# Dense layer of a fused attention and mixture-of-experts kernel: weight conversion spread over other places of the activation, and the low operand's matmuls put last

## The chip, the cores and the metric

The kernel runs on one core of a Trainium2 chip. TensorE (PE) multiplies matrices into PSUM banks, VectorE (DVE), ScalarE (ACT) and GpSimd (POOL) work on elements, and SyncE (SP) issues most transfers. Each engine takes its own instructions in the order in which the program gives them, and waits for the others by semaphores. The metric is the device time of one execution in microseconds (us); lower is better.

## The reference

Three layers follow one another. The change lies in the second, which is dense:

```python
def _moe_ref(x, w_in, w_out):            # x: 1536 x 512, w_in: 512 x 2048, w_out: 2048 x 512
    h = x @ w_in
    beta = 1.0
    neg = h <= -beta
    pos = h >= beta
    g = np.where(pos, h, np.where(neg, 0.0, (h + beta) ** 2 / (4.0 * beta)))
    return (g @ w_out).astype(np.float32)
```

Ahead of it stands a bucketed attention that makes x (2 batches, 8 heads, 768 rows), and behind it a layer with 8 experts of which each token takes two.

## The kernel before

**Tiles and steps.** The 1536 tokens are cut into 4 chunks `c` of 384, and the 2048 hidden columns into 16 blocks `f` of 128. A step is one pair (c, f). The first 32 steps take chunks 0 and 1 in turn, so that block f is used in steps 2f and 2f+1; then chunk 2 takes its 16 blocks, then chunk 3. Every operand is held as two parts, a rounded high part and a low rest, so that a product is three matmuls: high by high, high by low, low by high.

**What a step does.** `hidden` (L552) gives TensorE 12 matmuls of 384 columns into one of two banks (L561; the third of them is the first that reads the low part `w[:, 1]` of the block's weights). Then the activation goes from engine to engine: ACT `relu` into `ga` (L567), DVE `clip` of `ga` (L570, both inputs in SBUF), DVE `max` of the bank and `ga` (L573, one input in PSUM), ACT `round` into the high part `gh` (L574), POOL `rest` into the low part `gl` (L575). `out` (L578) belongs to the step two earlier (`lag = 2`) and gives TensorE 9 matmuls of 512 columns (L584): for each of three output banks `gh` by high, `gh` by low, `gl` by high.

**Weight conversion.** The weights arrive as 64-bit words in `R`. They are turned into the two float parts in eight pieces (`Weights.steps`, L299), which go through a scratch tile `TB` with two halves, block j using half j mod 2: ACT `abs` (L315), DVE `clamp` (L316), DVE `shift` (L317), four DVE `merges` (L311), and the `split`, which is an ACT copy (L307) and a POOL subtraction (L308) that writes the low part. Blocks 0 to 2 are converted during attention. Blocks j = 3 to 15 are converted within the dense steps; block j starts at step s = 2j-4. So each pair of steps carries one whole conversion beside two activations.

**Order.** The order on every engine is that in which the Python code emits instructions; there is no scheduler. Steps 0 and 1 are emitted among the last instructions of attention. Before the change `hidden` takes one list `extra` and cuts it: its first two pieces go behind `relu`, the third behind `clip`, and those left behind `rest`. Even step s carries the first seven pieces, and odd step s+1 the split.

Of the kernel before, what the change touches and what calls it, by code (L numbers as in the profile page):

```python
# [47 lines left out]
def cols(i, n):  # L48
    return slice(i * n, (i + 1) * n)
# [19 lines left out]
class Attention:  # L69
# [175 lines left out]
    def run(self, hooks, drain):  # L245

        lag, nt, plan = 4, self.nt, {}
        for a in range(2):
            for i, j in enumerate((1, 1, 2, 3 + 4 * a, 3, 4)):
                plan.setdefault(j + 4 * a, []).append((self.prep, a, i))  # L250
            plan.setdefault(5 + 6 * a, []).append((self.proj, a, f"x{a}"))
        self.start()
        done = 0
        for t in range(nt + 4):
            pr, j = divmod(t, 12)
            if t < nt:
                self.scores(t)
            if t >= lag:
                self.transposes(t - lag)
            self.soft(t)  # L260
            self.flush(2 if j < 2 else 1)
            if pr < 7:
                for f, a, i in plan.get(j, []):
                    f(2 * pr + 2 + a, i)
            if pr < 8 and j == 0:
                self.load_v(pr)
            if pr < 6 and j in (6, 11):
                self.load(2 * pr + 4 + (j == 11))
            for f in hooks.get(t, []):
                f()  # L270
            if t >= lag + 6:
                self.values(*divmod(t - lag - 6, 6))
                done += 1
            if t >= nt:
                drain(t - nt)
        while done < nt:
            self.values(*divmod(done, 6))
            done += 1
        self.flush()
# [263 lines left out]
class Dense:  # L543
# [8 lines left out]
    def py(self, c):  # L552
        return self.banks[5:8] if c == 1 else self.banks[2:5]

    def hidden(self, i, c, f, extra):
        nc, p, w = self.nc, self.banks[i % 2][:, :HT], self.wt.W[f]
        V, A = nc.vector, nc.scalar
        n = 0
        for k in range(4):
            for a, x in ((0, 0), (0, 1), (1, 0)):  # L560
                nc.tensor.matmul(p, w[:, a, cols(k, 128)], self.X[c][:, x, k], start=n == 0, stop=n == 11)  # L561
                n += 1
        a = self.sb.tile([128, HT], F32, name="ga", bufs=2)
        gh = self.sb.tile([128, HT], F32R, name="gh", bufs=3)
        gl = self.sb.tile([128, HT], F32R, name="gl", bufs=3)
        self.G[c, f] = gh, gl
        A.activation(a, p, AF.Relu, bias=self.half[:, 0:1], scale=0.5)  # L567
        for e in extra[:2]:
            e()
        V.scalar_tensor_tensor(a, a, 1.0, a, op0=ALU.min, op1=ALU.mult)  # L570
        for e in extra[2:3]:
            e()
        V.tensor_tensor(a, p, a, op=ALU.max)  # L573
        A.activation(gh, a, AF.Copy)  # L574
        nc.gpsimd.tensor_sub(gl, a, gh.bitcast(F32))  # L575
        for e in extra[3:]:
            e()

    def out(self, c, f):
        gh, gl = self.G.pop((c, f))  # L580
        w = self.wt.W[f]
        for t in range(3):
            for i, (g, a) in enumerate(((gh, 0), (gh, 1), (gl, 0))):
                self.nc.tensor.matmul(self.py(c)[t], g[:, cols(t, 128)], w[:, a, 512:1024],  # L584
                                      start=f == 0 and i == 0, stop=f == NF - 1 and i == 2)

    def run(self, convert, late, rows):

        lag, g, wt, yT = 2, self.gate, self.wt, self.yT
        order = [(c, f) for f in range(NF) for c in range(2)] + [(c, f) for c in (2, 3) for f in range(NF)]  # L590

        def stages(s, n):

            for t in range(n):
                at(s + t, lambda t=t: g.transposes(t, g.tp, yT))
                at(s + t + 1, lambda t=t: g.logits(t, yT))
            s += n
            for i, f in ((0, g.noise_a), (1, g.noise_b), (2, g.noise_c), (2, g.top2), (3, g.weights), (4, g.rank), (4, g.slot)):
                at(s + i, f)
            for t in range(n):  # L600
                at(s + 5 + t // 3, lambda t=t: g.hot(t))
                at(s + 6 + t // 3, lambda t=t: g.place(t))

        plan = {}

        def at(i, f):
            plan.setdefault(i, []).append(f)

        split = {}
        for i in range(4 * NF + lag):  # L610
            if i < 4 * NF:
                extra = []
                for j in [j for j, s in convert.items() if s == i]:
                    st = wt.steps(j)
                    extra += st[:-1]
                    split.setdefault(i + 1, []).append(st[-1])
                extra += split.get(i, [])
                self.hidden(i, *order[i], extra)
            if i >= lag:
                c, f = order[i - lag]  # L620
                self.out(c, f)
                if f == NF - 1 and 0 < c < 3:
                    if c == 1:
                        g.take(0, rows(0))
                        for t in range(6):
                            g.evac(t, self.banks[2 + t])
                        stages(i + 1, 6)
                    else:
                        g.take(6, rows(2))
                        for t in range(3):  # L630
                            g.evac(t, self.py(2)[t])
                        stages(i + 1, 3)
            for e in plan.pop(i, []) + late.get(i, []):
                e()
            yield i


class Experts:
# [10 lines left out]
    def __init__(self, nc, tc, ident, gate, W, prefetch, banks, xd, idx, out, TB, XT):  # L649
        self.nc, self.tc, self.ident, self.gate, self.W, self.prefetch = nc, tc, ident, gate, W, prefetch  # L650
        self.xd, self.idx, self.dst, self.banks = xd, idx, out, banks
        self.V, self.A, self.G, self.T = nc.vector, nc.scalar, nc.gpsimd, nc.tensor
        flat = TB.rearrange("p a b -> p (a b)")
        self.xr = [flat[:, cols(b, XW)] for b in range(3)]
        self.XT = [XT]
# [102 lines left out]
    def rows(self, j, o):  # L758

        n, il, sent = self.blocks(j, o), self.il[o % 2], []  # L760
        gt = self.columns(j, o)[1]

        def one(b):
            if b == 0:
                self.V.tensor_tensor(il[:, :n], self.idx[:, self.col(j, 3 * o, n)], self.apart[:, :n], op=ALU.max)
            self.put(b, gt[:, b:b + 1], il[:, b:b + 1], sent)
        return [lambda b=b: one(b) for b in range(n)]
# [77 lines left out]

@with_exitstack
def tile_bucketed_attention__then__moe__then__moe2(ctx, tc, qk, vv, pp, wio, wg, wn, noise, w12, out):
    nc = tc.nc
    const = ctx.enter_context(tc.tile_pool(name="const", bufs=1))
# [177 lines left out]
```

## Time and profile before

| what | value |
|---|---|
| time, median of 3 runs (lowest to highest) | 961.88 us (960.09 to 964.64) |
| the profiled execution's own time | 965.52 us |
| its span on the core | 963.7 us, so 1.8 us lie around the span |
| busy share of the span: PE, DVE, ACT, POOL | 91%, 60%, 45%, 41% |
| dense steps 2 to 63 | 263.6 to 562.6 us |
| weight conversion within the dense steps (L307 to L317) | 266.6 to 393.9 us |

The busy shares are means over the whole span, so they hide a stretch in which another engine leads. PE's busy time counts overlapping matmuls and does not say that it runs at its peak.

### The profile page before, as it was taken

Reading aid. Unit: us, or ns where it says so; the run is one execution under the profiler, and the core shown is the slowest. Engines: PE = TensorE matmul, PEld = TensorE weight load, DVE = VectorE, ACT = ScalarE, POOL = GpSimd, SP = SyncE. Lnnn points to the kernel's source line nnn. Section 1 sums busy time; section 2 is a strip of 40 time slices with the busy share of each in tenths; the row PEclk is TensorE's granted clock in tenths of the full one; section 3 lists DMA queues with packets and bytes.
Section 4 is the critical chain, followed back from the end, with each engine's and each line's share of the span. In section 5 each row is a group of like instructions: output and inputs, shape, how many; then the busy total and the mean of one; then the engine's idle time right before and its main releaser. Section 6 shows DMA issues by size and latency. Waiting matters only on the chain.

```text
span 963.7 us, 13751 instructions
## 1 busy us (share of the span) xinstructions
PE 875.0 (91%) x4846; PEld 716.0 (74%) x4846; DVE 579.7 (60%) x1215; ACT 433.1 (45%) x786; POOL 393.8 (41%) x403
## 2 busy tenths in 40 slices
PE   5999999999999898999999999978988968989873
PEld 3666666666687777899899888867877857878763
DVE  7899999988378787532926725326333445354352
ACT  4787787788534434333334432214322334334240
POOL 7777776784244545322221320332123143140332
PEclk8999999999999999999999999979999979999987
DMA  4439212112560000000501421346535376483742
GB/s 148 157 107 265 83 50 83 50 50 94 201 274 1 1 0 1 1 1 1 198 1 63 145 69 36 70 81 159 165 79 134 124 213 167 164 223 101 202 91 37
DMA packets 39883, 98.49 MB, mean 102 GB/s; under 512 B 6080, under 2 KB 15296, under 8 KB 37696
## 3 DMA queue, kind: packets, MB, share of 16 engines
q1 hardware_dynamic: 30688, 73.69, 22.8%
q0 software_dynamic: 8912, 22.50, 11.2%
q8 instruction: 94, 1.54, 0.7%
q14 instruction: 45, 0.37, 0.1%
q10 hardware_dynamic: 144, 0.39, 0.1%
HBM read 80.00 MB, written 16.58 MB: 100 GB/s over the span
## 4 chain that ended last, share of the span: by engine, by line
PE 40%; DMA 33%; DVE 15%; ACT 5%; issue 3%; another core or an unknown queue 2%; POOL 1%; POOLq 0%; SPq 0%; ACTq 0%; DVEq 0%
DMA xr<-xd,idx 16%; DMA out_dram<-yT,il 9%; DMA xm<-xd,idx 8%; PE b L561 7%; PE b L584 7%; PE bank_x L217 6%; PE bank_t L209 5%; PE s L178 4%; DVE TB L311 4%; PE s L180 3%; DVE ga L570 2%; DVE st L189 2%; PE b L714 2%; PE b L720 2%
## 5 line engine op out<-in xcount | busy, mean ns | idle before, releaser
L714 PE MATMUL b<-W,hT 128*128 128x512 f32 x648 | 176.9, 416 | 39.3 <-issue 34.6
L714 PEld LDWEIGHTS b<-W,hT 128*128 128x128 f32 x648 | 122.6, 198 | 65.7 <-issue 41.5
L688 POOL DMA_INDIRECT out_dram<-yT,il x33 | 52.4, 1589 | 258.9 <-DVE yT L752 256.4
L748 DVE SCALAR_TENSOR_TENSOR hT<-b,hT 128x384 fp32r<-128x384 f32 x88 | 49.0, 556 | 178.8 <-ACT hT L747 177.2
L747 ACT ACTIVATE hT<-b 128x384 fp32r<-128x384 f32 x88 | 43.3, 492 | 236.2 <-PE b L720 235.5
L561 PE MATMUL b<-X,W 128*128 128x384 f32 x768 | 147.3, 340 | 0.0
L575 POOL TENSOR_TENSOR gl<-ga,gh 128x384 fp32r<-128x384 f32 x64 | 75.2, 1177 | 165.2 <-ACT gh L574 126.5
L561 PEld LDWEIGHTS b<-X,W 128*128 128x128 f32 x768 | 135.0, 189 | 6.2 <-issue 1.8
L200 POOL TENSOR_SCALAR p<-p,st 128x768 f32<-128x768 f32 x96 | 98.1, 1022 | 63.1 <-DVE st L195 51.4
L584 PE MATMUL b<-W,gh 128*128 128x512 f32 x384 | 120.7, 395 | 0.0
L197 ACT ACTIVATE p<-s,st 128x768 f32<-128x768 f32 x96 | 95.5, 995 | 41.7 <-DVE st L195 34.6
L189 DVE TENSOR_REDUCE st<-s 128x1 f32<-128x768 f32 x96 | 91.7, 955 | 17.7 <-PE s L180 16.1
L720 PEld LDWEIGHTS b<-XT,W 128*128 128x128 f32 x576 | 88.9, 197 | 5.3 <-issue 1.8
L720 PE MATMUL b<-XT,W 128*128 128x256 f32 (+2 forms) x576 | 91.7, 314 | 1.2 <-issue 1.1
L570 DVE SCALAR_TENSOR_TENSOR ga<-ga 128x384 f32<-128x384 f32 x64 | 46.9, 733 | 74.8 <-ACT ga L567 74.8
L932 DVE TENSOR_TENSOR W<-stage,W 128x1024 fp32r<-128x1024 f32 x64 | 78.3, 1224 | 22.0 <-ACT W L931 22.0
L584 PE MATMUL b<-W,gl 128*128 128x512 f32 x192 | 77.6, 404 | 12.8 <-POOL gl L575 12.8
L210 ACT ACTIVATE pT<-bank_t 128x384 f32<-128x384 f32 x192 | 83.4, 488 | 8.9 <-PE bank_t L209 7.9
L217 PE MATMUL bank_x<-pT,vt 128*64 128x384 f32 x384 | 81.8, 510 | 0.4 <-DVE KM L165 0.3
L720 PE MATMUL b<-XA,W 128*128 128x384 f32 (+1 forms) x480 | 81.5, 323 | 0.0
L574 ACT ACTIVATE gh<-ga 128x384 fp32r<-128x384 f32 x64 | 33.6, 525 | 105.9 <-DVE ga L573 105.9
L209 PE MATMUL bank_t<-ident,p 128*128 128x128 f32 x576 | 79.4, 274 | 1.4 <-ACT pT L210 1.4
(171 smaller groups left out, 1303.3 us busy)
## 6 DMA issues: line engine op xcount, KB each, us to landing
stage<-in_w_dram SPq DMA_DIRECT2D x64, 512.0 KB, 4.4
R<-in_wio_dram SPq DMA_DIRECT2D x16, 1024.0 KB, 7.3
raw<-in_qk_dram SPq DMA_DIRECT2D x15, 768.0 KB, 4.3
out_dram<-z SPq DMA_DIRECT2D x15, 256.0 KB, 4.9
vt<-in_vv_dram SPq DMA_DIRECT2D x8, 384.0 KB, 4.8
xd<-TB SPq DMA_DIRECT2D x3, 780.0 KB, 3.7
xd<-z SPq DMA_DIRECT2D x3, 260.0 KB, 6.0
xd<-rows SPq DMA_DIRECT2D x1, 780.0 KB, 6.0
```

The source lines that it names most:

```text
L189: V.tensor_reduce(st[:, 0:1], s[:, :, :HT], axis=AX.XY, op=ALU.min)
L197: self.A.activation(p.rearrange("p (a b) -> p a b", a=2), s[:, :, :HT], AF.Exp, bias=st[:, 2:3], scale=st[:, 3:4], accum_out=st[:, 5:6])
L200: self.G.tensor_scalar(self.P[t - 1], self.P[t - 1], ps[:, 5:6], 1.0, op0=ALU.mult, op1=ALU.mult)
L209: self.T.transpose(b[:, cols(j, 128)], p[:, cols(3 * g + j, 128)], self.ident)
L210: self.A.activation(self.PT[u, s][:, cols(g, 3), cols(i, 128)], b[:, :HT].rearrange("p (j q) -> p j q", j=3), AF.Copy)
L217: self.T.matmul(xp[cols(s, 64), :HT], self.vt[pr][:, s, kt, :], self.PT[u, s][:, kt, :], start=kt == 0, stop=kt == 5)
L561: nc.tensor.matmul(p, w[:, a, cols(k, 128)], self.X[c][:, x, k], start=n == 0, stop=n == 11)
L575: nc.gpsimd.tensor_sub(gl, a, gh.bitcast(F32))
L584: self.nc.tensor.matmul(self.py(c)[t], g[:, cols(t, 128)], w[:, a, 512:1024], start=f == 0 and i == 0, stop=f == NF - 1 and i == 2)
L714: self.T.matmul(self.banks[2 + b], h[:, a, cols(b, 128)], w2[:, x, 512:1024], start=i == LAG and n == 0, stop=i == LAG + 7 and n == 2)
L720: self.T.matmul(p, w[:, a, cols(k, 128)], X[:, x, k, :N], start=n == 0, stop=n == 11)
L932: nc.vector.tensor_sub(w[:, 1], d, w[:, 0].bitcast(F32))
```

## The change

`hidden` takes four lists in place of one and runs them at four places: `early` ahead of `relu`, `amid` behind `relu`, `mid` behind `clip`, `late` behind `rest`. `run` hands the eight pieces of block j to steps s-1 to s+2: abs to step s-1 (amid), clamp to s (mid), shift to s+1 (late), the four merges to s+2 (early) and the split to s+2 (amid). In `out` the two loops change places.

```diff
-    def hidden(self, i, c, f, extra):
+    def hidden(self, i, c, f, early, amid, mid, late):
...
         self.G[c, f] = gh, gl
+        for e in early:
+            e()
         A.activation(a, p, AF.Relu, bias=self.half[:, 0:1], scale=0.5)
-        for e in extra[:2]:
+        for e in amid:
             e()
         V.scalar_tensor_tensor(a, a, 1.0, a, op0=ALU.min, op1=ALU.mult)
-        for e in extra[2:3]:
+        for e in mid:
             e()
         V.tensor_tensor(a, p, a, op=ALU.max)
         A.activation(gh, a, AF.Copy)
         nc.gpsimd.tensor_sub(gl, a, gh.bitcast(F32))
-        for e in extra[3:]:
+        for e in late:
             e()
...
-        for t in range(3):
-            for i, (g, a) in enumerate(((gh, 0), (gh, 1), (gl, 0))):
+        for i, (g, a) in enumerate(((gh, 0), (gh, 1), (gl, 0))):
+            for t in range(3):
                 self.nc.tensor.matmul(self.py(c)[t], g[:, cols(t, 128)], w[:, a, 512:1024],
...
+            for n, (d, place) in enumerate([(-1, 1), (0, 2), (1, 3), (2, 0), (2, 0), (2, 0), (2, 0), (2, 1)]):
+                conv.setdefault(s + d, ([], [], [], []))[place].append(lambda j=j, n=n: wt.steps(j)[n]())
```

Line numbers in the changed kernel are 2 higher from `relu` on (L569 relu, L572 clip, L575 max, L576 round, L577 rest, L586 the matmuls of `out`).

On DVE, steps 3 to 5 before the change (`b1` is the bank of odd steps, `b0` of even ones, `R4` the words of block 4):

```order
L570 SCALAR_TENSOR_TENSOR ga_3037<-ga_3037 128x384
L573 TENSOR_TENSOR ga_3037<-b1_2854,ga_3037 128x384
L316 TENSOR_SCALAR TB_72<-TB_72 128x1024
L570 SCALAR_TENSOR_TENSOR ga_3069<-ga_3069 128x384
L317 TENSOR_SCALAR TB_72<-TB_72 128x1024
L573 TENSOR_TENSOR ga_3069<-b0_2853,ga_3069 128x384
L311 SCALAR_TENSOR_TENSOR TB_72<-R4_2598,TB_72 128x512 x4
L570 SCALAR_TENSOR_TENSOR ga_3105<-ga_3105 128x384
L573 TENSOR_TENSOR ga_3105<-b1_2854,ga_3105 128x384
```

The clamp, shift and merges of block 4 all stand in the even step 4. On DVE in the changed kernel, steps 3 to 5:

```order
L572 SCALAR_TENSOR_TENSOR ga_3032<-ga_3032 128x384
L575 TENSOR_TENSOR ga_3032<-b1_2854,ga_3032 128x384
L317 TENSOR_SCALAR TB_72<-TB_72 128x1024
L311 SCALAR_TENSOR_TENSOR TB_72<-R3_2596,TB_72 128x512 x4
L572 SCALAR_TENSOR_TENSOR ga_3063<-ga_3063 128x384
L316 TENSOR_SCALAR TB_72<-TB_72 128x1024
L575 TENSOR_TENSOR ga_3063<-b0_2853,ga_3063 128x384
L572 SCALAR_TENSOR_TENSOR ga_3100<-ga_3100 128x384
L575 TENSOR_TENSOR ga_3100<-b1_2854,ga_3100 128x384
L317 TENSOR_SCALAR TB_72<-TB_72 128x1024
L311 SCALAR_TENSOR_TENSOR TB_72<-R4_2598,TB_72 128x512 x4
```

The shift and merges of block 4 have moved from the even step to behind the next odd one, and the clamp has moved from ahead of the clip to behind it.

On PE, `hidden` of step 8 and the `out` behind it before the change (W_3109 is the weights of block 4):

```order
L561 MATMUL b_2853<-X_68,W_3109 128x384 [waits DVE_49]
L561 MATMUL b_2853<-X_68,W_3109 128x384 x11
L584 MATMUL b_2855<-W_3041,gh 128x512 [waits Activation_49]
L584 MATMUL b_2855<-W_3041,gh 128x512
L584 MATMUL b_2855<-W_3041,gl 128x512 [waits Pool_49]
L584 MATMUL b_2856<-W_3041,gh 128x512 x2
L584 MATMUL b_2856<-W_3041,gl 128x512
L584 MATMUL b_2957<-W_3041,gh 128x512 x2
L584 MATMUL b_2957<-W_3041,gl 128x512
```

In the changed kernel the same place reads (W_3139 is the weights of block 4):

```order
L561 MATMUL b_2853<-X_68,W_3139 128x384 [waits DVE_49,Activation_49]
L561 MATMUL b_2853<-X_68,W_3139 128x384
L561 MATMUL b_2853<-X_68,W_3139 128x384 [waits Pool_49]
L561 MATMUL b_2853<-X_68,W_3139 128x384 x9
L586 MATMUL b_2855<-W_3071,gh 128x512 [waits Activation_49]
L586 MATMUL b_2856<-W_3071,gh 128x512
L586 MATMUL b_2958<-W_3071,gh 128x512
L586 MATMUL b_2855<-W_3071,gh 128x512
L586 MATMUL b_2856<-W_3071,gh 128x512
L586 MATMUL b_2958<-W_3071,gh 128x512
L586 MATMUL b_2855<-W_3071,gl 128x512 [waits Pool_49]
```

The wait of `out` for POOL has moved from its third matmul to its seventh, and `hidden` of an even step now has waits of its own for ACT (first matmul) and for POOL (third), which come from the split.

## Rows read from the trace of the kernel before

**Rows 1.** Waits from 262 to 405 us: who waited for whom, total us, times, longest.
```profile
PE b L584 <- POOL gl L575: 12.8, 12, 1.1
```

**Rows 2.** The chain of waits from 286 to 396 us, its share by line.
```profile
by line: DVE TB L311 29.4%; DVE ga L570 14.1%; DVE TB L316 10.4%; ACT TB L315 10.3%; ACT W L307 9.3%; issue 8.9%; ACT ga L567 5.7%; DVE ga L573 5.5%; PE b L584 4.5%; PE b L561 1.9%; DVE TB L317 0.6%; ACT gh L574 0.2%; ACTq L307 0.2%
```

**Rows 3.** Timeline of PE, `hidden` of steps 3, 4, 30: start, us, operation.
```profile
267.90 2.25 PE L561 MATMUL b<-X,W 128*128 128x384 f32 x12
272.07 2.25 PE L561 MATMUL b<-X,W 128*128 128x384 f32 x12
...
396.91 2.25 PE L561 MATMUL b<-X,W 128*128 128x384 f32 x12
```

**Rows 4.** Timeline of ACT, steps 9 and 10: start, us, [idle before <- releaser].
```profile
292.79 1.06 ACT L307 ACTIVATE W<-TB 128x1024 fp32r<-128x1024 f32 x1 [2.29 <-DVE TB L311]
293.79 0.53 ACT L574 ACTIVATE gh<-ga 128x384 fp32r<-128x384 f32 x1
294.22 0.57 ACT L567 ACTIVATE ga<-b,half 128x384 f32<-128x384 f32 x1
294.69 1.12 ACT L315 ACTIVATE TB<-R 128x1024 f32<-128x1024 f32 x1
```

**Rows 5.** Timeline of DVE, steps 9 to 11.
```profile
292.62 0.54 DVE L570 SCALAR_TENSOR_TENSOR ga<-ga 128x384 f32<-128x384 f32 x1
...
295.84 1.05 DVE L316 TENSOR_SCALAR TB<-TB 128x1024 f32<-128x1024 f32 x1 [2.08 <-ACT TB L315]
296.81 1.34 DVE L570 SCALAR_TENSOR_TENSOR ga<-ga 128x384 f32<-128x384 f32 x1
298.08 0.68 DVE L317 TENSOR_SCALAR TB<-TB 128x1024 int32<-128x1024 int32 x1
298.68 0.54 DVE L573 TENSOR_TENSOR ga<-b,ga 128x384 f32<-128x384 f32 x1
299.15 3.30 DVE L311 SCALAR_TENSOR_TENSOR TB<-R,TB 128x512 int32<-128x512 int32 x4
302.37 0.54 DVE L570 SCALAR_TENSOR_TENSOR ga<-ga 128x384 f32<-128x384 f32 x1
```

**Rows 6.** Timeline of POOL: the subtraction of the split in step 9.
```profile
293.93 2.41 POOL L308 TENSOR_TENSOR W<-TB,W 128x1024 fp32r<-128x1024 f32 x1 [2.38 <-ACT W L307]
```

**Rows 7.** Timeline of DVE in step 2, with POOL idle.
```profile
267.70 0.69 DVE L316 TENSOR_SCALAR TB<-TB 128x1024 f32<-128x1024 f32 x1 [2.87 <-ACT TB L315]
268.31 0.55 DVE L570 SCALAR_TENSOR_TENSOR ga<-ga 128x384 f32<-128x384 f32 x1
268.78 0.69 DVE L317 TENSOR_SCALAR TB<-TB 128x1024 int32<-128x1024 int32 x1
```

**Rows 8.** Timeline of POOL, ACT and DVE after the last split.
```profile
391.46 2.40 POOL L308 TENSOR_TENSOR W<-TB,W 128x1024 fp32r<-128x1024 f32 x1 [2.38 <-ACT W L307]
...
391.75 0.57 ACT L567 ACTIVATE ga<-b,half 128x384 f32<-128x384 f32 x1
392.35 1.93 DVE L570 SCALAR_TENSOR_TENSOR ga<-ga 128x384 f32<-128x384 f32 x1 [1.06 <-ACT ga L567]
...
393.82 1.31 POOL L575 TENSOR_TENSOR gl<-ga,gh 128x384 fp32r<-128x384 f32 x1
394.31 0.56 DVE L573 TENSOR_TENSOR ga<-b,ga 128x384 f32<-128x384 f32 x1
```

**Rows 9.** Timeline of PE, `out` of one step with no wait.
```profile
403.20 0.63 PE L584 MATMUL b<-W,gh 128*128 128x512 f32 x2
403.66 0.40 PE L584 MATMUL b<-W,gl 128*128 128x512 f32 x1
403.90 0.63 PE L584 MATMUL b<-W,gh 128*128 128x512 f32 x2
```

**Rows 10.** Stretches: us; busy PE, PEld, DVE, ACT, POOL; granted clock; DMA share, GB/s.
```profile
286.00:396.90 110.90, 98.10 (x476) 84.46 (x475) 87.39 (x113) 44.25 (x68) 60.01 (x36) 1.00 0.00 1
410.00:480.00 70.00, 70.00 (x400) 63.68 (x400) 33.87 (x113) 24.16 (x43) 15.24 (x15) 1.00 0.17 61
```

More of the change, by code (lines that the diff above doesn't have):

```diff
@@ L607, in at @@
             plan.setdefault(i, []).append(f)
-        split = {}
+        conv = {}
+        for j, s in convert.items():
+            for n, (d, place) in enumerate([(-1, 1), (0, 2), (1, 3), (2, 0), (2, 0), (2, 0), (2, 0), (2, 1)]):
+                conv.setdefault(s + d, ([], [], [], []))[place].append(lambda j=j, n=n: wt.steps(j)[n]())
         for i in range(4 * NF + lag):
             if i < 4 * NF:
[L612 to L618, printed above, removed]
+                self.hidden(i, *order[i], *conv.get(i, ([], [], [], [])))
             if i >= lag:
```

## The prediction

> **What bounds the kernel now.** I read the waits of the dense stretch first. TensorE, the busiest engine of the page, loses time there in one place: `out` waits for `gl` 12 times, 12.8 us in total [rows 1]. Taken alone this says that `gl` is taken too early, or that POOL is too slow. The chain of waits over the same stretch says otherwise: TensorE's lines hold only 4.5% and 1.9% of it, and the rest is DVE and ACT work on weights and activation [rows 2]. So I looked for a loop between these two engines, in the timelines of ACT and DVE over one pair of steps [rows 4, 5].
>
> It is there, and it closes. The split's copy starts at 292.79; behind it in ACT's queue come round (293.79), relu of the next even step (294.22) and abs of the next block (294.69). DVE has been idle for 2.08 us until that abs ends, then takes clamp (295.84), clip (296.81), shift (298.08), max (298.68), merges (299.15), and the next clip may issue at 302.37. The next split's copy needs these merges. From clip to clip, 292.62 to 302.37, that is **9.75 us for a pair of steps**. TensorE alone needs 4.17 us for a step (267.90 to 272.07) [rows 3], 8.34 for a pair. Its waits for `gl` are only where the loop's lateness reaches it: POOL's subtraction of the split stands ahead of `gl` in its queue.
>
> **The change part by part.** Nothing is added or removed; all instructions are moved.
>
> *Low operand last in `out`.* It lets `gl` come four matmuls later, 4 x 0.23 = 0.9 us in each step. While the loop sets the pace this only moves the waiting, so I count it at 0; it would count where `gl` alone is late. It costs bank changes: each matmul now goes to another bank than the one before, 9 changes a step against 3. Two matmuls into one bank start 0.46 us apart from the next change (403.20 to 403.66), the change itself 0.24 (403.66 to 403.90) [rows 9]: 0.23 against 0.24, at most 0.01 for a change, so 384 changes more (6 x 64 steps) cost between 0 and 3.8 us; nearest is 0, since the difference is the rounding of the rows.
>
> *The loop is cut.* abs moves to the odd step before, so clamp finds its input ready. DVE's 2.08 us of idle time go, and the split's copy no longer stands between merges and clamp. What is left is a new loop, and to find its length one row decides: clip at 392.35 took 1.93 us beside the split's subtraction on POOL, against 0.55 alone [rows 7, 8]. It ended 0.42 after POOL's end (393.86 to 394.28), and `rest`, which was asked for at 393.82, ended 0.85 after clip. The max that followed ran 0.56 beside that `rest`, its ordinary 0.54 [rows 5, 8]. So clip and POOL's work exclude each other, and max is free. Clamp shows the same (1.05 against 0.69), merges too: four take 3.22 from issue to issue (299.15 to 302.37) with a `rest` inside [rows 5, 7].
>
> Now a pair in the new order, with 0 where the merges have been issued and clip of the even step can start:
> - clip 0 to 0.47, clamp to 1.08 (spacings 0.47 and 0.61 [rows 7]), then max;
> - the split's copy starts 0.17 behind the clip's place (292.62 to 292.79), POOL's subtraction 1.14 later at 1.31 (292.79 to 293.93), and takes 2.41, to 3.72 [rows 4 to 6];
> - clip of the odd step has its relu by about 2.8, waits for POOL, and ends at 3.72 + 0.42 = 4.14;
> - `rest` of the even step ends at 4.14 + 0.85 = 4.99. Max runs beside it; shift is held until then, and has passed by about 5.5 (its spacing is 0.60: 298.08 to 298.68 [rows 5]);
> - the merges with the odd step's `rest` inside, 3.22: the next clip can start at **8.7**.
>
> So DVE and POOL together set 8.7 us a pair, a little over TensorE's 8.34 and 1.05 under the old loop. That shift is held has no row; the nearest is clamp, the same operation at the same size and time (0.69, 0.69 [rows 7]), which was held, so I take it as held. If it is not, it runs beside `rest`, the merges start near 5.2 and the pair is 8.4. The other end: if POOL takes `rest` directly behind the subtraction, clip of the odd step ends at 3.72 + 0.85 + 0.42 = 4.99, max and shift follow, merges start at 6.07 and the pair is 9.3.
>
> The Trainium skill, page SBUF — State Buffer, section "Who interferes with whom", names `tensor_scalar` among the DVE operations that can hold the port pair shared with GpSimd, for the whole instruction. By that rule shift is held and the pair is 8.7; were it exempt, 8.4. No run here shows a shift beside POOL work, so the rule stands on the side of the value that I took from clamp's row.
>
> *Where the lateness goes next.* The subtraction now runs in step 2j-2 and writes the low weights that `hidden` of step 2j reads in its third matmul; the order shows the new wait there. In TensorE's own pace that matmul comes 5.74 us after clip's undisturbed start (8.34 + 0.35 - 2.95, with clip 2.25 + 0.10 + 0.60 behind the start of `hidden` [rows 3, 8]). The subtraction is done at 3.72 + 0.05, so DVE may be 2.0 late before TensorE waits. It starts 0.7 late and gains 0.36 a pair, so from the fourth or fifth pair on `hidden` waits about 0.36 us a pair, 3 us in all. The seventh matmul of `out` needs `gl` of the even step at 4.99, long after: there is no wait there.
>
> **Sum.** Step 3's `hidden` starts at 267.90 as before; its relu follows at 270.25, clip 270.85, max 271.45, shift 271.92, merges 272.52, and with 3.22 the first clip behind merges is at 275.7. Twelve pairs of 8.7 later, at 380.1, the last block's merges are done. Its subtraction ends 3.72 later, and `hidden` of step 30 can start at 380.1 + 3.77 - 0.35 = 383.5. Before it started at 396.91 [rows 3]. **Gain 13.4 us.** TensorE is then back to back (70.00 busy of 70.00 from 410 to 480 [rows 10]) and the conversion is over, so I see nothing that takes the gain back. abs of block 3 moves into attention's end, where ACT waits for DVE's max anyway. Transfers hide nothing and delay nothing: from 286 us on they move 1 GB/s [rows 10]. From the profiled execution's 965.52 the sum gives 952.1; that execution lies 3.64 above the median of 961.88, from which it is **948.5 us**, the predicted time.
>
> **Rivals.**
> - *TensorE sets the pace* (shift free, pair 8.4). The lateness stays under 2.0, `hidden` of step 30 starts at 272.07 + 13 x 8.34 = 380.5, gain 16.4, 945.5 us. Against it: the port work has to fit with no gap.
> - *POOL keeps the port* (pair 9.3). The last merges are done at 275.7 + 12 x 9.3 = 387.3, step 30 starts at 390.7, gain 6.2, 955.7 us. Against it: at 393.86 the waiting clip went ahead of the queued `rest` [rows 8].
> - *No change.* The gain is made and given back behind step 33, for instance in the gathers of the expert layer: 960 to 964. Against it: no timed event stands there, only work that shifts as a whole.
> - *Slower: changing banks costs.* If each of the 384 added changes costs more than (13.4 + 4.8) / 384 = 0.047 us, the kernel is slower by over 0.5%; at 0.06 it loses 23 us, wins 13.4, and takes 971.5. Against it: 0.01 at most in [rows 9].
>
> **How the numbers follow.** Chances: forecast (pair 8.5 to 9.0) 0.62, TensorE's pace 0.14, POOL keeps the port 0.14, no change 0.07, slower 0.03. The forecast's own range is a pair of 8.5 to 9.0 (gain 16 to 9.8, up to 952.1) with 1.5 us of scatter between runs. The range 944.5 to 956 takes in the first two rivals and leaves out the others. A difference of 0.5% (4.8 us) is about what can be told from no change: faster 0.90, same 0.07, slower 0.03.
>
> **What would show it.** Right: merges start every 8.6 to 8.8 us; the wait of `out` for `gl` is under 1 us in total; a new one, the third matmul of `hidden` on POOL's L308, grows from mid-stretch to about 3 us; clip of the odd step takes about 1.3 us on average; step 30 starts near 383.5. Wrong: merges every 8.34 (shift free) or 9.3 (`rest` first), clamp still idle behind abs, DVE ops of one length beside POOL work, or `out` matmuls more than 0.24 apart.

## The result, and the profile after

The changed kernel took 952.76 us (median of 4 runs, 948.55 to 955.30) beside 961.82 us for the kernel before: a ratio of 0.990, 95% interval 0.985 to 0.994, so 9 us faster by the medians. The profiled execution took 953.94 us, its span is 952.2 us. Timed again beside the experiments (e4 below), the same kernel took 950.82 us against 963.16 us, a ratio of 0.987 (0.984 to 0.990), 12.3 us. The prediction was 948.5 us from a gain of 13.4 us; both intervals hold its ratio of 0.986.

Where the time came from is seen in `hidden` of steps 3 and 30, which answer to [rows 3]. The timeline of PE in the changed kernel:

```profile
264.14 2.35 PE L561 MATMUL b<-X,W 128*128 128x384 f32 x12
...
268.41 2.25 PE L561 MATMUL b<-X,W 128*128 128x384 f32 x12
...
383.78 2.49 PE L561 MATMUL b<-X,W 128*128 128x384 f32 x12
...
549.22 0.86 PE L586 MATMUL b<-W,gl 128*128 128x512 f32 x3
```

From step 3 to step 30 it takes 115.4 us, where it took 129.0 (267.90 to 396.91 [rows 3]): 13.6 us less. I call the time from the first matmul of step 2 to the end of the last matmul of `out` the dense part. It ends at 550.1 (549.22 + 0.86), 550.1 - 264.1 = 286.0 us behind its start, 13.0 less than before (562.6 - 263.6 = 299.0). What lies behind the dense part took 402.1 us in this profile and 401.1 before. Over the ten profiles of this study it took between 395.9 and 404.0 us, in no visible relation to what was changed, so single times scatter by some us there, and the dense part of a profile tells more than the whole time.

The waits from 262 to 405 us in the changed kernel, to be read beside [rows 1]:

```profile
ACT TB L315 <- POOL W L308: 10.6, 11, 1.1
...
PEld b L561 <- POOL W L308: 2.9, 9, 0.3
```

No line of `out` for `gl` is left among them. In its place stands the new wait that the prediction put there: `hidden` for the low weights, 9 times, 2.9 us in all (predicted: from the fourth or fifth pair on, about 3 us). ACT's abs waits for POOL 11 times, and nobody waits for abs any more. Before, the same window had this line, which is now gone:

```profile
DVE TB L316 <- ACT TB L315: 27.9, 13, 2.9
```

The chain of waits over the conversion (286 us to the start of step 30), to be read beside [rows 2]:

```profile
by line: PE b L561 50.8%; PE b L586 49.2%; issue 0.1%
```

TensorE's lines held 6.4% of the chain and now hold all of it. That doesn't mean that TensorE runs at its own pace: this view counts the short waits of its weight loads for POOL as TensorE's own. `hidden` of steps 21 to 23 shows them:

```profile
344.82 2.26 PE L561 MATMUL b<-X,W 128*128 128x384 f32 x12
...
349.02 2.54 PE L561 MATMUL b<-X,W 128*128 128x384 f32 x12
...
353.50 2.26 PE L561 MATMUL b<-X,W 128*128 128x384 f32 x12
```

The odd step takes 4.20 us (344.82 to 349.02), the even one, which waits, 4.48 (349.02 to 353.50). Together they are 8.68, the pace of DVE and POOL. These two in one pair of steps, DVE first, to be read beside [rows 5]:

```profile
345.84 0.55 DVE L572 SCALAR_TENSOR_TENSOR ga<-ga 128x384 f32<-128x384 f32 x1
346.31 0.68 DVE L316 TENSOR_SCALAR TB<-TB 128x1024 f32<-128x1024 f32 x1
346.91 0.55 DVE L575 TENSOR_TENSOR ga<-b,ga 128x384 f32<-128x384 f32 x1
348.52 1.39 DVE L572 SCALAR_TENSOR_TENSOR ga<-ga 128x384 f32<-128x384 f32 x1 [1.06 <-ACT ga L569]
349.94 0.56 DVE L575 TENSOR_TENSOR ga<-b,ga 128x384 f32<-128x384 f32 x1
350.42 0.93 DVE L317 TENSOR_SCALAR TB<-TB 128x1024 int32<-128x1024 int32 x1
351.38 3.21 DVE L311 SCALAR_TENSOR_TENSOR TB<-R,TB 128x512 int32<-128x512 int32 x4
354.52 0.55 DVE L572 SCALAR_TENSOR_TENSOR ga<-ga 128x384 f32<-128x384 f32 x1
```

and POOL in the same pair:

```profile
347.09 2.40 POOL L308 TENSOR_TENSOR W<-TB,W 128x1024 fp32r<-128x1024 f32 x1 [3.53 <-PE b L561]
349.45 1.34 POOL L577 TENSOR_TENSOR gl<-ga,gh 128x384 fp32r<-128x384 f32 x1
351.22 1.02 POOL L577 TENSOR_TENSOR gl<-ga,gh 128x384 fp32r<-128x384 f32 x1 [0.43 <-POOL gl L577]
```

From clip to clip (345.84 to 354.52) a pair takes 8.68 us; the prediction said 8.7. Every step of its list is there: the subtraction runs from 1.25 to 3.65 on that clock (said: 1.31 to 3.72), clip of the odd step waits for it and ends at 4.07 (4.14), `rest` ends at 4.95 (4.99), and shift, for which the prediction had gone by clamp's row, takes 0.93 in place of 0.68 and ends 0.56 behind that `rest`. So shift is held too.

The two engines might also only slow each other and not exclude each other. No run was made for this, but the rows tell: clip asks 0.89 us after the subtraction has started in [rows 8] and 1.43 after it here, ends 0.42 behind the subtraction both times, and the subtraction takes 2.40 both times. An operation that only ran slower would end later the later it starts.

### The profile page after: what moved, and what is told of

The parts are those of the page before. It is cut to its first block, busy times and chain, and to the rows that moved or that the text cites. A ratio compares the mean times of both kernels' runs of the same rounds, so it can differ in the third digit from the quotient of the medians.

```text
span 952.2 us, 13762 instructions
## 1 busy us (share of the span) xinstructions
PE 872.6 (92%) x4846; PEld 714.7 (75%) x4846; DVE 577.4 (61%) x1215; ACT 436.4 (46%) x786; POOL 388.1 (41%) x403
## 4 chain that ended last, share of the span: by engine, by line
PE 50%; DMA 34%; DVE 8%; another core or an unknown queue 2%; issue 2%; ACT 2%; POOL 1%; POOLq 0%; SPq 0%; DVEq 0%; ACTq 0%
DMA xr<-xd,idx 16%; PE b L561 12%; PE b L586 12%; DMA out_dram<-yT,il 9%; DMA xm<-xd,idx 8%; PE bank_x L217 7%; PE bank_t L209 5%; PE s L178 4%; PE s L180 3%; DVE st L189 2%; PE b L714 2%; PE b L720 2%; PE bank_x L158 1%; PE b L386 1%
## 5 line engine op out<-in xcount | busy, mean ns | idle before, releaser
L577 POOL TENSOR_TENSOR gl<-ga,gh 128x384 fp32r<-128x384 f32 x64 | 69.6, 1089 | 143.2 <-ACT gh L576 122.6
L572 DVE SCALAR_TENSOR_TENSOR ga<-ga 128x384 f32<-128x384 f32 x64 | 46.0, 719 | 91.1 <-ACT ga L569 91.1
L586 PE MATMUL b<-W,gh 128*128 128x512 f32 x384 | 99.8, 395 | 0.0
L586 PEld LDWEIGHTS b<-W,gh 128*128 128x128 f32 x384 | 71.2, 188 | 11.5
L720 PEld LDWEIGHTS b<-XA,W 128*128 128x128 f32 x480 | 76.4, 192 | 4.1 <-issue 1.0
```

Of the source, the lines that this page charges most:

```text
L720: self.T.matmul(p, w[:, a, cols(k, 128)], X[:, x, k, :N], start=n == 0, stop=n == 11)
```

## The experiments

Two theories stood against each other. **Port**: DVE work with operands in SBUF alone (the memory that holds the tiles; the banks are in PSUM) and POOL work exclude each other, and the pair is as long as what they need one after the other, if every engine keeps its order. **Queue**: the pair is set by DVE's own queue and its waits for ACT, and POOL has time to spare. A third question was what the order in `out` is worth by itself. The time of the kernel before that e1 to e4 are compared with is 963.16 us, that of e5 to e8 962.82.

**e1: low operand last, alone** (the kernel before, with the loops of `out` changed places):

```diff
-        for t in range(3):
-            for i, (g, a) in enumerate(((gh, 0), (gh, 1), (gl, 0))):
+        for i, (g, a) in enumerate(((gh, 0), (gh, 1), (gl, 0))):
+            for t in range(3):
```

> The kernel before with one part of the change alone: the two loops of out changed places, so that gl is taken in matmuls 7 to 9. Theory (the loop of ACT and DVE sets 9.75 us a pair, TensorE's wait for gl is only where it shows): same time as before within 1 us, merges still every 9.75 us, step 30 still starts near 397, the 12.8 us of waiting move to other matmuls. Rival (the wait for gl is a cost of its own): 12 waits of about 1.07 us lose 0.9 us each, so 9 to 11 us faster, near 951. Price of a bank change, if any: slower by up to 3.8 us.

Measured: 963.37 us against 963.16, a ratio of 1.001 (0.999 to 1.003). Two of PE's waits from 262 to 405 us:

```profile
PE b L561 <- DVE ga L573: 5.7, 11, 0.5
...
PE b L584 <- POOL gl L575: 2.4, 10, 0.3
```

The merges of two blocks on DVE, and below them `hidden` of step 30:

```profile
328.48 3.30 DVE L311 SCALAR_TENSOR_TENSOR TB<-R,TB 128x512 int32<-128x512 int32 x4
...
338.25 3.31 DVE L311 SCALAR_TENSOR_TENSOR TB<-R,TB 128x512 int32<-128x512 int32 x4
```

```profile
396.20 2.28 PE L561 MATMUL b<-X,W 128*128 128x384 f32 x12
```

TensorE's wait for `gl` has fallen from 12.8 to 2.4 us, and other waits stand one group further on: `hidden` now waits for the bank that the late max has not yet read. The merges still come every 9.77 us (328.48 to 338.25). A shorter wait is no shorter loop. What is won is won once, when the loop ends: step 30 starts at 396.20 in place of 396.91, and of these 0.7 us the dense part keeps 0.4 (298.6). Nor does changing the bank with each matmul cost anything that the interval shows.

**e2: the moved conversion, alone** (the changed kernel with the old order in `out`, the diff of e1 backwards).

> The changed kernel with the old order in out (gl in matmuls 3, 6 and 9), so that the moved conversion works alone. Theory: the same as the changed kernel within 1 us, since gl of the even step is ready 2.9 us before the third matmul of its out even at the largest lateness; pair 8.7 us, step 30 near 383.8, no wait for gl. Rival (the two parts need each other): 12 waits for gl come back and 5 to 10 us of the gain are lost.

Measured: 952.25 us, a ratio of 0.989 (0.986 to 0.993). PE's only waits for POOL from 262 to 405 us:

```profile
PEld b L561 <- POOL W L308: 2.8, 9, 0.4
```

No wait for `gl` came back, and the dense part takes 285.8 us (286.0 and, in e4, 286.2 in the changed kernel). So the moved conversion is the whole gain.

**e3: the rest of the odd steps on DVE** (from the changed kernel):

```diff
-        nc.gpsimd.tensor_sub(gl, a, gh.bitcast(F32))
+        rest = lambda: (V if i in self.moved else nc.gpsimd).tensor_sub(gl, a, gh.bitcast(F32))
+        if i in self.moved:
+            self.moved[i].insert(2, rest)
+        else:
+            rest()
...
+        self.moved = {s + 1: conv[s + 2][0] for s in convert.values()}
```

> The changed kernel with the rest (gl) of the 13 odd steps 3 to 27 on DVE in place of POOL, put between the second and third merge. Same result. Theory (what excludes each other on DVE and POOL sets the pair): the port work falls by 0.87 + 0.55 for POOL's rest and the merge held behind it, and rises by 0.60 + 0.47, so 8.7 becomes 8.3 to 8.4 us although DVE has 0.47 us more to do; TensorE then sets the pace, the third matmul of hidden no longer waits for the split, and the time is 2 to 3 us under the changed kernel's. Rival (DVE's own queue sets the pair): 8.7 + 0.47 = 9.15 us a pair, 5 to 6 us slower than the changed kernel.

Measured: 949.12 us, a ratio of 0.986 (0.983 to 0.989). By time alone it can't be told from e4, but its dense part takes 283.4 us against 286.2 in e4, 2.7 less. DVE from the clip of the odd step to that of the even one, with `rest` (L577) between the merges:

```profile
329.75 1.40 DVE L572 SCALAR_TENSOR_TENSOR ga<-ga 128x384 f32<-128x384 f32 x1 [1.06 <-ACT ga L569]
...
331.66 0.92 DVE L317 TENSOR_SCALAR TB<-TB 128x1024 int32<-128x1024 int32 x1
332.62 1.29 DVE L311 SCALAR_TENSOR_TENSOR TB<-R,TB 128x512 int32<-128x512 int32 x2
333.83 0.55 DVE L577 TENSOR_TENSOR gl<-ga,gh 128x384 fp32r<-128x384 f32 x1
334.30 1.29 DVE L311 SCALAR_TENSOR_TENSOR TB<-R,TB 128x512 int32<-128x512 int32 x2
335.50 0.55 DVE L572 SCALAR_TENSOR_TENSOR ga<-ga 128x384 f32<-128x384 f32 x1
```

On its PE, the start of the dense part, two `hidden` a pair apart, and the end of the dense part:

```profile
263.88 2.35 PE L561 MATMUL b<-X,W 128*128 128x384 f32 x12
...
364.51 2.26 PE L561 MATMUL b<-X,W 128*128 128x384 f32 x12
...
372.91 2.26 PE L561 MATMUL b<-X,W 128*128 128x384 f32 x12
...
546.43 0.86 PE L590 MATMUL b<-W,gl 128*128 128x512 f32 x3
```

DVE has more to do and is done sooner: the merges with the `rest` among them take 2.88 (332.62 to 335.50) where they took 3.14 with POOL's (351.38 to 354.52), and the next step follows TensorE's 8.40 us, with no wait of `hidden` for the low weights left. This speaks for the port and against the queue.

**e4: the changed kernel again.**

> The changed kernel as it is, timed beside the three others and in more rounds. Theory: the dense part gains 12.5 to 13.4 us and nothing behind it gives any back, so 948 to 950 if before is at 961.9, a ratio of 0.985 to 0.988. Rival (a part of the gain is lost behind the dense part): a ratio of 0.990 or more, and in the profile the experts' part longer than before by 3 us or more.

Measured: 950.82 us against 963.16, a ratio of 0.987 (0.984 to 0.990); dense part 286.2 us, what lies behind it 399.3. The dense part gains 12.8 us and the time 12.3, so nothing that stands out of the scatter is given back behind it.

**e5: abs early, alone of the moved conversion** (from the changed kernel, so with the low operand last; the table gives each of the eight pieces its step and its place, where 0 is ahead of relu, 1 behind it, 2 behind clip, 3 behind `rest`):

```diff
-[(-1, 1), (0, 2), (1, 3), (2, 0), (2, 0), (2, 0), (2, 0), (2, 1)]
+[(-1, 1), (0, 1), (0, 2), (0, 3), (0, 3), (0, 3), (0, 3), (1, 1)]
```

> Of the moved conversion only abs goes a step earlier (behind the split's copy of the odd step); clamp, shift, merges and split stand where they stood before; out takes the low operand last. Theory (DVE and POOL exclude each other, and every engine keeps its order): clamp no longer waits for abs at 2.08 us of idle DVE, but it now meets the split's subtraction on POOL. With 0 at the clip of the odd step: subtraction 1.31 to 3.72, clamp to 4.27, rest to 5.12, clip to 5.54, shift, max at 6.06, merges 6.53 to 9.75. So the pair stays at 9.7 to 9.8 us and the time that of before within 1.5 us. Rival (what counts is that DVE waited for ACT, and POOL doesn't matter): the pair loses about 2 us, TensorE sets 8.34, and the time is 12 to 16 us under before.

Measured: 958.92 us against 962.82, a ratio of 0.997 (0.994 to 1.000): 3.9 us less, where at most 1.5 was expected. DVE and, below it, POOL in one pair:

```profile
320.42 0.55 DVE L572 SCALAR_TENSOR_TENSOR ga<-ga 128x384 f32<-128x384 f32 x1
...
322.65 1.97 DVE L316 TENSOR_SCALAR TB<-TB 128x1024 f32<-128x1024 f32 x1 [1.09 <-ACT TB L315]
324.54 1.37 DVE L572 SCALAR_TENSOR_TENSOR ga<-ga 128x384 f32<-128x384 f32 x1
...
326.90 3.31 DVE L311 SCALAR_TENSOR_TENSOR TB<-R,TB 128x512 int32<-128x512 int32 x4
330.13 0.55 DVE L572 SCALAR_TENSOR_TENSOR ga<-ga 128x384 f32<-128x384 f32 x1
```

```profile
321.67 2.40 POOL L308 TENSOR_TENSOR W<-TB,W 128x1024 fp32r<-128x1024 f32 x1 [2.32 <-ACT W L307]
```

The pair takes 9.71 us (320.42 to 330.13; expected 9.7 to 9.8, the rival's 8.34). The pair came as expected, the time did not. Clamp still waits for abs, but less (1.09 us in place of 2.08), and then takes 1.97 us in place of 1.05, since it ends only 0.55 behind the subtraction. The dense part is 2.7 us shorter than before (296.3). The pair explains 0.5 of this (12 x 0.04), and what e1 won once another 0.4 to 0.7. The first merges start at 268.62 in place of 269.85 with abs out of their way, in a profile whose step 2 started 0.4 later: 1.6 more. The expectation left the last two out; that they add up in this way is an argument and was not tried by a run.

**e6: merges and split late, alone of the moved conversion** (from the changed kernel):

```diff
-[(-1, 1), (0, 2), (1, 3), (2, 0), (2, 0), (2, 0), (2, 0), (2, 1)]
+[(0, 1), (0, 1), (0, 2), (2, 0), (2, 0), (2, 0), (2, 0), (2, 1)]
```

> Of the moved conversion only merges and split go two steps on (ahead of the relu of the even step, and behind it); abs, clamp and shift stand where they stood before; out takes the low operand last. Theory: abs now stands behind the split's copy in the same step and clamp ahead of clip, so the clip of the even step waits for both and for the subtraction: with 0 at the end of the merges, copy 0.17, abs 1.17 to 2.3, subtraction 1.31 to 3.72, clamp to 4.27, clip 4.7, shift 5.3, max 5.8, round, relu 6.9, rest and clip of the odd step 7.8, merges from 8.35 to 11.5. A pair of 11.3 to 11.6 us, step 30 near 417, slower than before by 17 to 21 us. Rival (pieces out of the even step's chain always help): 3 to 12 us faster than before.

Measured: 988.53 us, a ratio of 1.026 (1.019 to 1.032), slower. POOL from one subtraction to the next:

```profile
311.83 2.38 POOL L308 TENSOR_TENSOR W<-TB,W 128x1024 fp32r<-128x1024 f32 x1 [2.33 <-ACT W L307]
316.99 1.01 POOL L577 TENSOR_TENSOR gl<-ga,gh 128x384 fp32r<-128x384 f32 x1 [2.77 <-ACT gh L576]
319.69 1.38 POOL L577 TENSOR_TENSOR gl<-ga,gh 128x384 fp32r<-128x384 f32 x1 [1.69 <-issue]
323.39 2.41 POOL L308 TENSOR_TENSOR W<-TB,W 128x1024 fp32r<-128x1024 f32 x1 [2.32 <-ACT W L307]
```

A pair takes 11.56 us. Step 30 starts at 419.09 (expected near 417) and the dense part is 22.8 us longer than before; what lies behind it took 2.9 more in this profile, which is within its scatter. So the merges' new place is no gain by itself: with abs, clamp and shift left where they were, the same move costs more than the whole change wins.

**e7: the rest of the odd steps twice on POOL** (from the changed kernel):

```diff
-        nc.gpsimd.tensor_sub(gl, a, gh.bitcast(F32))
+        for _ in range(2 if i in range(3, 28, 2) else 1):
+            nc.gpsimd.tensor_sub(gl, a, gh.bitcast(F32))
```

> The changed kernel with the rest (gl) of the 13 odd steps 3 to 27 done twice by POOL, one behind the other, with the same output. POOL has 2.41 + 3 x 1.0 = 5.4 us of work in a pair of 8.7, so it is not full. Theory (what excludes each other on DVE and POOL sets the pair): the second one holds up the merges by another 0.8 to 0.9 us, the pair becomes 9.5 to 9.6, step 30 comes near 393.5, 9 to 11 us slower than the changed kernel. Rival (DVE's own queue and its waits for ACT set the pair; POOL has time to spare): same time as the changed kernel.

Measured: 961.26 us against 962.82, a ratio of 0.998 (0.995 to 1.002): by time no gain is left. The dense part takes 296.1 us, 9.9 more than in e4 and still 2.9 less than before. Clip to clip on DVE, POOL's work in the same pair, then PE's waits for POOL:

```profile
333.32 0.54 DVE L572 SCALAR_TENSOR_TENSOR ga<-ga 128x384 f32<-128x384 f32 x1
...
338.84 4.01 DVE L311 SCALAR_TENSOR_TENSOR TB<-R,TB 128x512 int32<-128x512 int32 x4
342.78 0.55 DVE L572 SCALAR_TENSOR_TENSOR ga<-ga 128x384 f32<-128x384 f32 x1
```

```profile
334.57 2.39 POOL L308 TENSOR_TENSOR W<-TB,W 128x1024 fp32r<-128x1024 f32 x1 [2.93 <-ACT W L307]
336.92 1.34 POOL L578 TENSOR_TENSOR gl<-ga,gh 128x384 fp32r<-128x384 f32 x1
338.64 2.46 POOL L578 TENSOR_TENSOR gl<-ga,gh 128x384 fp32r<-128x384 f32 x2 [0.38 <-ACT gh L576]
```

```profile
PEld b L561 <- POOL W L308: 13.4, 12, 1.2
PE b L561 <- POOL W L308: 9.5, 12, 0.9
```

The merges take 3.94 us (338.84 to 342.78) where they took 3.14, and the pair 9.46 (333.32 to 342.78; step 30 starts at 392.48). POOL is busy for 6.2 of these 9.46 us, so it has 3 us a pair to spare, and still the added operation lengthens the pair. This is the clearest result against the queue.

**e8: low weights last in `hidden`** (from the changed kernel):

```diff
-        for k in range(4):
-            for a, x in ((0, 0), (0, 1), (1, 0)):
+        for a, x in ((0, 0), (0, 1), (1, 0)):
+            for k in range(4):
```

> The changed kernel with the 12 matmuls of hidden in another order: the four that read the low weights come last (9 to 12) in place of 3, 6, 9 and 12, so their first is needed 6 x 0.174 = 1.04 us later. Theory (DVE is late by 0.36 us more in each pair, and TensorE meets this in the third matmul of hidden once it is over 2.0): the limit is 3.0, waits begin three pairs later and sum to about 1.7 in place of 2.8 us; step 30's work ends about 1 us sooner, which only the profile can tell (dense part 548.5 in place of 549.6 where it starts at 263.4); the time is the changed kernel's within its scatter. Rival (the wait lies elsewhere, in a bank or the high part): the same waits of 2.7 to 2.9 us.

Measured: 950.64 us, a ratio of 0.988 (0.982 to 0.994). PE's wait for POOL from 262 to 405 us:

```profile
PEld b L561 <- POOL W L308: 1.5, 5, 0.3
```

5 waits and 1.5 us in place of 9 and 2.7 to 2.9, and a dense part of 285.2 us, 0.9 less than in e4: the lateness grows and meets TensorE as worked out, with waits that begin four pairs later where three were expected.

## Why the prediction came out as it did

- *What bounds the kernel.* Right: the wait for `gl` was where the loop showed and not its cause. e1 took most of that wait away, and the time stayed where it was.
- *Low operand last, counted at 0.* Right within what can be measured: e2, which does without it, has a dense part as short. The 0.7 us won once at the loop's end (e1) was left out of the sum. The bank changes, bounded at 3.8 us, cost nothing that e1's interval shows (0.999 to 1.003).
- *The new pair of 8.7 us.* Right, 8.68. The step on which it rested, that clip, clamp and merges exclude POOL's work and max doesn't, was tried from both sides: less for POOL shortens the pair although DVE gets more (e3), more for POOL lengthens it by what DVE loses (e7). For clamp e5 shows it. The runs show that the two exclude each other; what in the chip makes them do so, they don't show. The value taken from clamp's row for shift was right too (0.93 in place of 0.68). The Trainium skill's rule on `tensor_scalar` (SBUF — State Buffer, "Who interferes with whom") agrees with that row. But the prediction was wrong that shift beside POOL work had no row: the trace of the kernel before has one in attention, shown below this list. Shift takes 1.28 us there in place of 0.68 and ends 0.55 behind another operation of POOL (67.34 and 66.79). So that shift is held could have been read before the result, and the pair of 8.4 had this row against it.
- *Who goes first behind the subtraction.* The waiting clip did, as in [rows 8]; the rival of 9.3 us did not occur.
- *Where the lateness goes.* Right in place and in total: 2.9 us in the third matmul of `hidden`, from step 14 on, which is the fifth conversion; e8 moved it. A single wait is 0.3 us where 0.36 was said, since TensorE's own pair is then 8.40 and not 8.34.
- *The sum.* Step 30 was put at 383.5 and came at 383.78 in a profile whose step 2 started 0.5 us later. The gain of 13.4 us shows as 13.0 in the dense part, 12.3 in e4's times and 9.1 in the first. The ten runs of the changed kernel lie between 948.29 and 955.30, and what lies behind the dense part differs by some 8 us over the profiles. The 1.5 us of scatter in the range understated this; of the terms that were mis-sized it is the largest.
- *TensorE's own pace* was put at 8.34 from one early step; in e3, where it leads, a pair takes 8.40, which takes 13 x 0.06 = 0.8 us off that rival's gain of 16.4. e3 gained 15.6 us in its dense part (299.0 against 283.4) and 14.0 in its times (963.16 against 949.12).

The row of shift beside POOL work in the kernel before, POOL above and DVE below:

```profile
65.88 0.91 POOL L200 TENSOR_SCALAR p<-p,st 128x768 f32<-128x768 f32 x1 [1.18 <-ACT pT L210]
```

```profile
66.06 1.28 DVE L317 TENSOR_SCALAR TB<-TB 128x1024 int32<-128x1024 int32 x1
```

The version with `rest` of the odd steps on DVE (e3) is ahead of both kernels by its dense part; by time it is ahead of the kernel before and not to be told from the changed one.

## What to carry to other kernels

When the busiest engine waits, follow the chain back until it closes on itself: a pace that is the same in every round and longer than each engine's own work points to a loop, and as in e1 a later use of what is waited for can move the wait without shortening the loop. For two engines that exclude each other, add up the time of the operations that exclude each other, not the busy time of either; an engine with a third of its time free can still set the pace. Pieces of a chain that are moved to other places have to be costed together: in the dense part abs alone won 2.7 us, the merges and the split alone lost 23, and all pieces together, clamp and shift with them, win 13. And before a term is taken from a similar operation, the whole trace is worth a search for the operation itself, other stages too: shift beside POOL stood in attention.

## What was not expected of the hardware

TensorE's step without waits took 4.17 us early in the dense part (267.90 to 272.07 [rows 3]) and 4.20 later (half of 364.51 to 372.91 in e3), at a granted clock of 1.00 in both. In the changed kernel and in e2, e3, e4 and e8 the pace changes at the same place, steps 10 and 11. No run here was made to tell why, and it stays open.
